# Another written order for a fused scan-attention and feed-forward kernel: scores in 20 places of TensorE's stream, not 44

## The chip, the cores and the metric

One NeuronCore of one Trainium2 chip runs the whole program; nothing is split over cores. The metric is the device time of one execution in microseconds (us), taken as the median of three runs. Engines: PE is TensorE (PEld its weight load), DVE is VectorE, ACT is ScalarE, POOL is GpSimd, SP is SyncE, whose queue issues nearly all DMAs.

## What is computed

A chunked linear attention with decay, then two feed-forward layers. In the reference's own terms, cut to what matters:

```python
for c in range(nc):                       # chunks of the sequence
    cum = np.cumsum(la, axis=-1)
    L = np.exp(cum[:, :, :, None] - cum[:, :, None, :]) * causal
    CB = np.einsum('bhin,bhjn->bhij', Cc, Bc)             # the scores
    y_intra = np.einsum('bhij,bhjd->bhid', CB * L, xc)
    y_inter = np.einsum('bhin,bhnd->bhid', Cc, state) * decay_to_i[:, :, :, None]
    y[:, :, sl] = y_intra + y_inter
    state = decay_full[:, :, None, None] * state + np.sum(Bx, axis=2)
h = np.maximum(np.maximum(x @ w1, x @ w2), x @ w3);  x = h @ w_out      # 256 -> 768 -> 256
gate = 1 / (1 + np.exp(-(x @ w_gate)));  out = gate * (x @ w_val) @ w_out   # 256 -> 1536 -> 256
```

There are 4 batches, 8 heads and 768 positions, so 3072 tokens of 256 features. Inputs are float32.

## The kernel before

The sequence is cut into 8 chunks of 96 positions, and the 32 pairs of batch and head into 8 groups of four, so the attention has 64 steps k = 8c + g. Each step is a **score** (`score`, L344 to L356), a **weighing** (`weigh`, L366 to L376) and, by fours from step 24 on, **outputs** (`outputs`, L378 to L388). A score is four matmuls. For k below 16 they are float32, from operands that ScalarE masks (`mask`, L338 to L341, words `k0` to `k15`); from chunk 2 on they are bfloat16 (L355), on operands `bi` and `cs` split in three parts (words `P`, `Q`) and spread by DMAs (words `Pd`). A score lands in a PSUM tile of the pool `psu`, which has three tiles under one tag, `up`. DVE's weighing (word `m`) multiplies it by the decay factors, and so frees the PSUM tile. The decay factors of two steps share a tile `dec`; it is loaded (word `Ld`) and turned into factors by two scans on DVE (words `D..a`, `D..b`, L303). `dec0` and `dec1` come from the input; the later ones come from a clipped copy `ad` that the kernel makes at its start (words `a`, `clip`, `astore`). Four buffers hold `dec` tiles, so load n waits for the weighings of tile n - 4. The scan needs a constant in PSUM, `delta`, which ACT copies (L273).

Outputs (word `y`, L385) are matmuls of 32 columns each. ACT rounds their result (`high`, word `H`), DVE takes the rest (`low`, word `X`), and four transposes on DVE (`turn`, word `T`) bring the state to the next chunk.

The first feed-forward layer runs beside the attention, on tiles of 512 tokens. Every float32 product is three matmuls on high and low halves of its operands. A word `G` issues the terms (high and low weight, high activation), a word `F` the third (low activation). So a `G` with its `F` is six matmuls of 512 columns (in the trace `u<-xt_hi` x4 and `u<-xt_lo` x2), into one PSUM tile of the same three. `E` (ACT), `U` and `V` (DVE) take the maximum over the three products and so free their tiles, `h` and `l` split it, and `N`, `O` are the six matmuls of the down projection (`o<-hi`, `o<-lo`). The words `Lwa`, `sga`, `rawa`, `stta`, `ra`, `adda`, `hia`, `loa` load and decode this layer's weights.

What is written by hand is `ORDER` (L52), a text of such words. `in_order` (L714) emits word after word, and ties each engine's instructions of a word behind that engine's instructions of the words before it. So the text fixes the order on every engine and on SP's queue, and between engines only data, semaphores and buffers decide. `ON_DVE` (L105) lists the words among `adda`, `loa`, `l` and `Q` that DVE does; the others of these kinds go to POOL. After the text come the last products of the first layer and the whole second layer (`ug`, `uv`, `o<-hi,w_d`), whose code isn't part of the change.

```python
def weigh(k):
    ...
        last[0] = dve.tensor_tensor(out=m[:, :, 0:CH], in0=ps[:, :, 0:CH], in1=dc[:, :, 1:LW],
                                    op=ALU.mult)
```

Of the kernel before, what the change touches and what calls it, by code (L numbers as in the profile page):

```python
# [52 lines left out]
LB0 K Lwa00#0 a clip LC0 pk delta Lwa00 sga00 rawa00 stta00 Ld0 clip0 k6 Ld1 k2 k4 D0b S2 ra00 k5  # L53
clip1 D1a m2 adda00 I0 astore hia00 Lb2 P20 k0 D0a k1 I1 I2 Lx00#0 Lx00 bx2 Q20 k3 D1b Ld2 D2b I3
I4 I5 I6 LC1 S0 m0 S3 k7 bx3 m3 bx0 S1 m1 P21 Ld3 S5 m5 k9 I7 k8 D2a bx1 Lwa01#0 Lwa01 k13 k11 S7
loa00 D3a D3b m7 Lx01#0 sga01 rawa01 S4 m4 S6 m6 y3 Q21 Lwa10#0 Lx01 bx4 stta01 ra01 y4 Ld4 D4a y0
y2 y1 H00 X00 D4b I8 I9 Lwa10 bx7 sga10 rawa10 stta10 k14 I10 I11 LB1 I12 k10 adda01 Ld5 bx5 y5
Lx10#0 Lx10 y7 bx6 y6 H01 Lwa11#0 Lwa11 D5b bx11 D5a S11 S10 m11 S9 ra10 S8 T00 bx10 m10 y11 y10
adda10 Ld6 hia01 m9 bx9 y9 m8 hia10 bx8 y8 H10 Ld7 sga11 rawa11 X01 ra11 Lwa20#0 Lwa20 sga20 X10
loa10 loa01 Lwa21#0 Lwa21 D7a rawa20 D6b S13 m13 G000 F000 G001 F001 stta11 adda11 E00 sga21  # L60
rawa21 U00 ra20 Lwa30#0 Lwa30 stta20 stta21 Lx11#0 Lx11 G002 F002 G010 F010 hia11 loa11 ra21 k12
Lwa31#0 sga30 Lwa31 V00 G011 F011 G012 F012 E01 D7b bx14 h00 adda20 bx15 S12 rawa30 U01 V01 Ld8
l00 hia20 Ld9 ra30 sga31 Lx20#0 Lx20 adda21 stta30 D6a hia21 m12 Lwa41#0 loa20 rawa31 ra31 N00 O00
stta31 loa21 Lwa40#0 Lwa40 adda30 hia30 G020 F020 loa30 adda31 G021 F021 P22 k15 G022 F022 T10 h01
D8a E02 U02 bx16 V02 Lwa41 sga41 Lwa50#0 Lwa50 sga40 S14 m14 rawa40 ra40 stta40 l01 hia31 adda40
hia40 Pd21#0 S15 rawa41 loa31 G030 F030 h02 bx12 E03 Pd22#0 Pd22 N01 O01 T01 bx13 D9a bx18 G031
F031 Pd21#1 m15 y15 y13 Pd21#2 ra41 D8b bx17 sga50 l02 stta41 adda41 rawa50 ra50 stta50 loa40 U03
hia41 y12 G032 F032 N02 O02 Pd20#0 Pd20#1 Pd20#2 Pd20#3 D9b V03 Pd20#4 G040 F040 loa41 Pd20 E04
Pd21 S19 m19 S17 m17 y14 Ld10 Lwa51#0 h03 S16 G041 F041 m16 adda50 hia50 loa50 Lwa51 sga51 rawa51
D10a l03 Lx21#0 Lx21 Ld11 Lx31#0 U04 S20 m20 ra51 G042 F042 V04 h04 S18 m18 G050 F050 E05 N03 O03  # L70
S22 Lb3 stta51 S23 adda51 hia51 bx19 y18 y16 D11a Ld12 D10b bx21 m22 loa51 y17 D11b m23 y19 H11
X11 G051 F051 S21 P30 G052 F052 l04 T11 bx23 y23 Lx31 m21 bx22 H20 X20 y21 U05 bx20 y20 y22 H21
Lx30#0 X21 Q30 V05 h05 Lx30 Pd30#0 D12a bx24 Lx41#0 Lx41 N04 O04 D12b bx25 Pd30#1 Pd30#2 G100 F100
T20 G101 F101 P31 Q31 E10 U10 G102 F102 V10 P32 l05 G110 F110 E11 N05 O05 f0 Pd30#3 Ld13 Ld14 D13b
D14a D13a G111 F111 h10 G112 F112 G120 F120 l10 N10 O10 U11 V11 G121 F121 h11 l11 Pd30#4 Pd30 bx27
E12 Pd32#0 Pd31#0 Pd31#1 Pd31#2 Pd31 Pd32 S27 m27 Lb4 U12 P40 G122 F122 V12 S24 D14b Pd40#0 bx29
m24 Q40 G130 F130 N11 O11 h12 l12 G131 F131 S25 m25 E13 G132 F132 U13 V13 S26 h13 l13 P41 Pd40#1
Pd40#2 Pd40#3 m26 N12 O12 Ld15 D15a D15b bx26 G140 F140 E14 S28 m28 G141 F141 Ld16 bx31 bx28 T21
Lx40#0 Q41 Pd40#4 bx30 P42 S29 G142 F142 U14 Lx40 m29 V14 S30 m30 G150 F150 E15 Ld17 D17a S31
Pd42#0 Pd42 G151 F151 Ld18 Pd40 y27 H30 m31 bx34 y31 H31 X31 D18b X30 D16a U15 G152 F152 Pd41#0  # L80
h14 l14 N13 O13 V15 h15 Ld19 D19b D16b D19a D18a G200 F200 E20 N14 O14 G201 F201 U20 G202 F202
bx33 Pd41#1 Pd41#2 bx32 Pd41 S33 m33 l15 N15 O15 Lb5 P50 Q50 P51 Pd51#0 bx37 Pd50#0 V20 G210 F210
E21 h20 l20 Q51 Pd51#1 T31 S32 m32 T30 Pd50#1 G211 F211 Ld20 S34 m34 f1 U21 G212 F212 V21 Pd51#2
bx36 S37 m37 D17b Lx51#0 G220 F220 E22 h21 l21 S35 m35 Lx50#0 G221 F221 U22 P52 S38 m38 N20 O20
G222 F222 S36 D20b D20a V22 h22 m36 G230 F230 E23 bx35 y35 H40 G231 F231 U23 Pd51 S39 G232 F232
Pd52#0 Pd50#2 Ld21 Pd50#3 m39 Pd50#4 Pd50 Lx50 bx38 l22 X40 bx40 bx39 V23 N21 O21 h23 Pd52 G240
F240 E24 S42 D21a m42 D21b N22 O22 Lb6 P60 Q60 G241 F241 U24 Lx51 S41 bx42 m41 P61 G242 F242 V24
h24 Ld22 Ld23 Pd60#0 Pd60#1 l23 Pd60#2 S40 m40 G250 F250 E25 S43 G251 F251 bx41 D22a m43 T40
Pd60#3 y39 H41 X41 Pd61#0 bx43 y43 H50 X50 G252 F252 Pd61#1 N23 O23 D22b Ld24 l24 Q61 U25 V25
Pd61#2 G300 F300 S45 m45 G301 F301 N24 O24 Ld25 D24a Lx60#0 bx45 P62 h25 l25 Pd62#0 Pd62 Pd60#4  # L90
D23a E30 U30 G302 F302 V30 S44 m44 N25 O25 G310 F310 D25b D23b S47 bx46 m47 D24b h30 Pd60 G311
F311 E31 U31 S46 m46 Lb7 bx44 Pd61 l30 G312 F312 Ld26 V31 P70 f2 bx47 S51 m51 G320 F320 h31 Pd70#0
Pd70#1 Q70 Pd70#2 Pd70#3 Pd70#4 Lx60 S49 P71 G321 F321 T41 D25a Ld27 y47 E32 m49 U32 Q71 P72 bx50
# [880 lines left out]
```

## Time and profile before

| | |
|---|---|
| median of three runs | 546.75 us (545.62 to 547.71) |
| the profiled execution | 546.38 us, its span 544.6 us |
| busy in the span | PE 523.3 us (96%), PEld 418.2, DVE 401.1 (74%), ACT 313.8, POOL 90.4 |
| chain that ended last | PE 82%, DVE 7%, DMA 5%, ACT 3%, issue 2% |
| granted TensorE clock | 1.00 over the span |

Attention and the first layer take the span up to about 208 us, the second layer the rest. A group of matmuls in the timeline has the start of its first one and the time to the end of its last one; matmuls overlap, so the pace of PE is read from one group's start to the next one's, not from the second column. A row of the waits says which engine and line stood idle, until whose work, for how many us in total, how often, and the longest. "issue" means that no wait is visible.

### The profile page before, as it was taken

Reading aid. Unit: us, or ns where it says so; the run is one execution under the profiler, and the core shown is the slowest. Engines: PE = TensorE matmul, PEld = TensorE weight load, DVE = VectorE, ACT = ScalarE, POOL = GpSimd, SP = SyncE. Lnnn points to the kernel's source line nnn. Section 1 sums busy time; section 2 is a strip of 40 time slices with the busy share of each in tenths; the row PEclk is TensorE's granted clock in tenths of the full one; section 3 lists DMA queues with packets and bytes.
Section 4 is the critical chain, followed back from the end, with each engine's and each line's share of the span. In section 5 each row is a group of like instructions: output and inputs, shape, how many; then the busy total and the mean of one; then the engine's idle time right before and its main releaser. Section 6 shows DMA issues by size and latency. Waiting matters only on the chain.

```text
span 544.6 us, 7902 instructions
## 1 busy us (share of the span) xinstructions
PE 523.3 (96%) x2897; PEld 418.2 (77%) x2898; DVE 401.1 (74%) x682; ACT 313.8 (58%) x551; POOL 90.4 (17%) x127
## 2 busy tenths in 40 slices
...
GB/s 209 289 308 214 211 158 164 162 151 138 204 182 139 222 17 201 186 46 148 78 40 0 2 0 1 1 40 39 2 0 1 0 1 78 1 0 0 2 0 78
DMA packets 33895, 50.53 MB, mean 93 GB/s; under 512 B 3392, under 2 KB 19904, under 8 KB 33856
## 3 DMA queue, kind: packets, MB, share of 16 engines
...
## 4 chain that ended last, share of the span: by engine, by line
PE 82%; DVE 7%; DMA 5%; ACT 3%; issue 2%; SPq 0%; POOL 0%; DVEq 0%; POOLq 0%; ACTq 0%
PE u L461 22%; PE o L851 17%; PE ug L820 15%; PE uv L820 15%; PE o L461 7%; PE y L385 2%; PE s L352 2%; DVE dec L303 2%; PE s L355 1%; DMA bc<-in_bch 1%; DMA bx<-in_bn 1%; DMA dec<-ad 1%; DVE t_a L609 1%; DVE mt L375 1%; DVE s L644 1%
## 5 line engine op out<-in xcount | busy, mean ns | idle before, releaser
L461 PE MATMUL u<-xt_hi,w_a 128*128 128x512 f32 x432 | 121.6, 402 | 1.7 <-DVE w_a L618 0.5
L820 PE MATMUL ug<-xt_hi,w_g 128*128 128x512 f32 x252 | 92.0, 390 | 0.3 <-ACT ug L823 0.2
L461 PEld LDWEIGHTS u<-xt_hi,w_a 128*128 128x128 f32 x432 | 77.3, 188 | 19.0 <-DVE w_a L618 1.4
L820 PE MATMUL uv<-xt_hi,w_v 128*128 128x512 f32 x252 | 91.1, 390 | 0.0
L851 PE MATMUL o<-hi,w_d 128*128 128x512 f32 x288 | 78.4, 389 | 0.0
L461 PE MATMUL u<-xt_lo,w_a 128*128 128x512 f32 x216 | 66.9, 391 | 0.4 <-DVE xt_lo L402 0.4
L303 DVE TENSOR_TENSOR_SCAN dec<-dec,delta 128x388 f32<-128x388 f32 x64 | 59.5, 949 | 4.5 <-DMA dec<-ad 4.3
L851 PEld LDWEIGHTS o<-hi,w_d 128*128 128x128 f32 x288 | 54.1, 188 | 11.3
L895 DVE TENSOR_TENSOR lo<-y,hi 128x512 fp32r<-128x512 f32 x72 | 49.2, 687 | 16.1 <-ACT hi L894 15.2
L820 PEld LDWEIGHTS ug<-xt_hi,w_g 128*128 128x128 f32 x252 | 47.3, 188 | 11.2 <-ACT ug L823 0.7
L820 PEld LDWEIGHTS uv<-xt_hi,w_v 128*128 128x128 f32 x252 | 47.3, 188 | 10.7 <-DVE y L828 0.4
L894 ACT CAST hi<-y 128x512 fp32r<-128x512 f32 x72 | 44.5, 620 | 13.2 <-DVE y L891 12.0
L820 PE MATMUL ug<-xt_lo,w_g 128*128 128x512 f32 x126 | 49.1, 389 | 0.0
L820 PE MATMUL uv<-xt_lo,w_v 128*128 128x512 f32 x126 | 49.0, 389 | 0.0
L891 DVE TENSOR_TENSOR y<-uv,y 128x512 f32<-128x512 f32 x36 | 24.8, 688 | 32.9 <-PE uv L820 32.5
L461 PEld LDWEIGHTS u<-xt_lo,w_a 128*128 128x128 f32 x216 | 40.5, 188 | 9.7 <-DVE xt_lo L402 0.9
L851 PE MATMUL o<-lo,w_d 128*128 128x512 f32 x144 | 45.6, 391 | 0.0
L825 ACT COPY sv<-uv 128x512 f32<-128x512 f32 x36 | 21.2, 588 | 34.9 <-PE uv L820 34.7
L375 DVE TENSOR_TENSOR mt<-s,dec 128x384 f32<-128x384 f32 x64 | 34.6, 549 | 8.8 <-PE s L355 7.2
L644 DVE TENSOR_TENSOR s<-u,s 128x512 f32<-128x512 f32 x50 | 34.1, 682 | 8.4 <-PE u L461 7.3
L828 DVE TENSOR_TENSOR y<-ug,y 128x512 f32<-128x512 f32 x36 | 24.8, 689 | 21.0 <-ACT y L825 15.0
L461 PE MATMUL o<-hi,w_a 128*128 128x512 f32 x144 | 39.6, 397 | 0.0
(107 smaller groups left out, 808.7 us busy)
## 6 DMA issues: line engine op xcount, KB each, us to landing
...
```

Source lines behind the costliest of these rows:

```text
L303: dve.tensor_tensor_scan(out=f, data0=f, data1=delta.rearrange("p u w -> p (u w)"), initial=0.0, op0=ALU.mult, op1=ALU.add)
L352: pe.matmul(ps[:, q, 0:CH], bcf[c][:, 128 * q:128 * q + 128], cm[:, k % MASKED, q], start=True, stop=True)
L375: last[0] = dve.tensor_tensor(out=m[:, :, 0:CH], in0=ps[:, :, 0:CH], in1=dc[:, :, 1:LW], op=ALU.mult)
L461: pe.matmul(ps, w[int(e == 1)], a_lo if e == 2 else a_hi, start=start, stop=stop)
L644: evict[1] = dve.tensor_tensor(out=s, in0=banks_of[t, m, 1 + (kind == "V")], in1=s, op=ALU.max)
L820: turn[0] = pe.matmul(ps, w, x, start=new and e == 0, stop=e == 2, skip_group_check=not new)
L825: evict[0] = act.copy(self.temp(1 if i == 6 else 2), ps)
L828: evict[1] = dve.tensor_tensor(out=self.t[k], in0=ps, in1=self.t[k], op=ALU.add)
L851: turn[0] = pe.matmul(acc2[t][d], w, x, start=n == 1 and e == 0, stop=n == M2 and e == 2)
L891: evict[1] = dve.tensor_tensor(out=g, in0=v, in1=g, op=ALU.mult)
L894: act.copy(hl[0], g)
L895: dve.tensor_tensor(out=hl[1], in0=g, in1=hl[0].bitcast(F32), op=ALU.subtract)
```

## The change

A new text `ORDER` and a new list `ON_DVE`. No function, size, tile or product changes. A few rows of the text:

```diff
-LB0 K Lwa00#0 a clip LC0 pk delta Lwa00 sga00 rawa00 stta00 Ld0 clip0 k6 Ld1 k2 k4 D0b S2 ra00 k5
-clip1 D1a m2 adda00 I0 astore hia00 Lb2 P20 k0 D0a k1 I1 I2 Lx00#0 Lx00 bx2 Q20 k3 D1b Ld2 D2b I3
+a Lwa00#0 K I0 I1 Ld0 Lwa00 sga00 clip0 pk clip I2 rawa00 stta00 LC0 k0 LB0 k3 delta D0b k4 D0a
+astore S0 Lx00#0 Lx00 bx1 Ld1 k7 k1 ra00 m0 I3 I4 I5 I6 I7 I8 adda00 hia00 clip1 D1b I9 D1a bx2
...
-ON_DVE = """Q20 loa10 adda20 adda21 loa21 adda40 l02 loa40 l05 l10 l11 l12 l21 l25 l35""".split()
+ON_DVE = """adda20 adda21 adda30 loa21 loa30 adda40 loa40 loa50 l04 Q31 l21 Q60 Q61 l23 l31 l34 l35""".split()
```

By the instruction order as built, the bfloat16 scores stood in 44 places of PE's stream with float32 products between them, and now stand in 20. Outputs that stand between scores of one place are counted with it. The three excerpts below are of that order; where an instruction is issued four times in a row, one row of it is shown.

First, TensorE in the fifth chunk. `s5_2` is the score of chunk 5, group 2; `u3_2_4_0` is a product of token tile 2; `o6_2_0` belongs to the down projection; `y1`, `y0` are outputs. Before:

```order
L355 MATMUL s5_2_1593<-cs5_1370,bi1_97 128x96
L461 MATMUL o6_2_0_1484<-hi3_2_2_1448,w_a21_538 128x512
...
L461 MATMUL u3_2_4_1_1613<-xt_hi_92,w_a40_623 128x512 x4
L461 MATMUL u3_2_4_1_1613<-xt_lo_93,w_a40_623 128x512 x2
L355 MATMUL s5_1_1622<-cs5_1370,bi1_97 128x96
L461 MATMUL u3_2_4_2_1630<-xt_hi_92,w_a41_695 128x512 x4
L461 MATMUL u3_2_4_2_1630<-xt_lo_93,w_a41_695 128x512 x2
L355 MATMUL s5_0_1647<-cs5_1370,bi1_97 128x96
L461 MATMUL u3_2_5_0_1656<-xt_hi_92,w_a50_770 128x512 x4
L461 MATMUL u3_2_5_0_1656<-xt_lo_93,w_a50_770 128x512 x2
L355 MATMUL s5_3_1664<-cs5_1370,bi1_97 128x96
```

and now:

```order
L460 MATMUL u3_2_4_2_1624<-xt_hi_92,w_a41_688 128x512 x4
L460 MATMUL u3_2_4_2_1624<-xt_lo_93,w_a41_688 128x512 x2
L460 MATMUL o6_2_0_1445<-hi3_2_3_1495,w_a31_620 128x512
...
L354 MATMUL s5_1_1639<-cs5_1362,bi1_97 128x96
L354 MATMUL s5_2_1645<-cs5_1362,bi1_97 128x96
L354 MATMUL s5_0_1651<-cs5_1362,bi1_97 128x96
L384 MATMUL y1_107<-mt7_105,xs4_1_1024 32x112 x4
...
L354 MATMUL s5_3_1677<-cs5_1362,bi1_97 128x96
L460 MATMUL u3_2_5_0_1690<-xt_hi_92,w_a50_702 128x512 x4
```

The four scores of that group, each alone between products before, stand around one set of outputs.

Second, SP's queue at the start of the program. `y1` is the scratch that takes the first chunk's B (512 columns) and C (384 columns), `a4` the decay input for the copy `ad`. Before:

```order
L576 DMA y1_91<-in_bch 128x512
L593 DMA raw_a00_137<-in_w1 128x2x256
L680 DMA a4_110<-in_ah 64x388
L574 DMA y1_91<-in_bch 128x384
L678 DMA pk_109<-in_pick 128x8
L593 DMA raw_a00_137<-in_w2 128x2x256
L287 DMA dec0_149<-in_ah 128x776
L287 DMA dec1_153<-in_ah 128x776
L683 DMA ad_108<-a4_110 64x388
```

and now:

```order
L679 DMA a4_110<-in_ah 64x388
L592 DMA raw_a00_112<-in_w1 128x2x256
L286 DMA dec0_142<-in_ah 128x776
L592 DMA raw_a00_112<-in_w2 128x2x256
L677 DMA pk_109<-in_pick 128x8
L573 DMA y1_91<-in_bch 128x384
L575 DMA y1_91<-in_bch 128x512
L682 DMA ad_108<-a4_110 64x388
...
L286 DMA dec1_172<-in_ah 128x776
```

`dec0` is the third load, not the seventh; B and C come after it; `dec1` comes after the store of `ad` and the first inputs x. On DVE the clip of `a4` now stands behind the clip of `dec0`, and on ACT the copy of `delta` behind the first weight and two masks.

Third, SP's queue where `dec17` to `dec19` are loaded; `cs4`, `bi0` are the spread operands of chunk 4. Before:

```order
L287 DMA dec16_1185<-ad_108 128x776
L294 DMA xs4_0_1193<-in_xh 128x512
L666 DMA cs4_1075<-parts4_1074 16x8x384
L294 DMA bx4_0_1194<-in_bn 128x256
L287 DMA dec17_1233<-ad_108 128x776
L666 DMA bi0_96<-parts4_1074 16x8x512
L666 DMA cs4_1075<-parts4_1074 16x8x384
L287 DMA dec18_1250<-ad_108 128x776
L666 DMA cs4_1075<-parts4_1074 16x8x384
L666 DMA bi0_96<-parts4_1074 16x8x512
L287 DMA dec19_1312<-ad_108 128x776
```

and now:

```order
L286 DMA dec16_1166<-ad_108 128x776
L665 DMA cs4_946<-parts4_945 16x8x384
L293 DMA xs5_0_1217<-in_xh 128x512
L293 DMA bx4_1_1025<-in_bn 128x256
L665 DMA bi0_96<-parts4_945 16x8x512
L286 DMA dec17_1263<-ad_108 128x776
L286 DMA dec18_1311<-ad_108 128x776
L286 DMA dec19_1314<-ad_108 128x776
```

The three loads stand together, ahead of the last spreading DMAs of chunk 4 instead of among them.

## Rows read from the trace of the kernel before

**Rows 1.** Busy time by stretch: from 11 us, from 77.6 us.

```profile
core 0: us, PE busy (x) PEld busy (x) DVE busy (x) ACT busy (x) POOL busy (x), PEclk, DMA share, GB/s
11.00:77.60 66.60, 61.30 (x487) 46.64 (x491) 63.72 (x101) 45.41 (x77) 39.38 (x48) 1.00 0.83 239
77.60:208.80 131.20, 128.98 (x961) 98.11 (x953) 104.07 (x180) 44.73 (x73) 46.33 (x63) 1.00 0.70 148
```

**Rows 2.** Waits of the weight load, 77.6 to 209 us: total, times, longest.

```profile
PEld L355 <- issue: 11.0, 38, 1.1
```

**Rows 3.** TensorE's timeline, 82 to 104 us: start, us, engine, line, operation.

```profile
83.43 1.07 PE L461 MATMUL u<-xt_hi,w_a 128*128 128x512 f32 x4
...
84.79 1.07 PE L461 MATMUL o<-hi,w_a 128*128 128x512 f32 x4
...
94.68 0.35 PE L355 MATMUL s<-cs,bi 96*128 96x96 bf16 x4
94.85 1.17 PE L461 MATMUL u<-xt_hi,w_a 128*128 128x512 f32 x4
...
96.30 1.07 PE L461 MATMUL o<-hi,w_a 128*128 128x512 f32 x4
```

**Rows 4.** TensorE's timeline, 186 to 212 us: two scores together, outputs.

```profile
198.39 0.51 PE L355 MATMUL s<-cs,bi 96*128 96x96 bf16 x8
198.73 1.17 PE L461 MATMUL u<-xt_hi,w_a 128*128 128x512 f32 x4
...
200.20 0.35 PE L355 MATMUL s<-cs,bi 96*128 96x96 bf16 x4
...
205.34 0.34 PE L355 MATMUL s<-cs,bi 96*128 96x96 bf16 x4
205.61 0.97 PE L385 MATMUL y<-mt,xs 128*32 128x112 f32 x32
206.52 1.20 PE L461 MATMUL u<-xt_hi,w_a 128*128 128x512 f32 x4
...
208.10 0.97 PE L385 MATMUL y<-mt,xs 128*32 128x112 f32 x32
```

**Rows 5.** TensorE's timeline, 104 to 131 us: two outputs in one stop, waits.

```profile
110.66 1.74 PE L385 MATMUL y<-mt,xs 128*32 128x112 f32 x64
112.33 1.20 PE L461 MATMUL u<-xt_hi,w_a 128*128 128x512 f32 x4
...
116.69 0.73 PE L461 MATMUL u<-xt_lo,w_a 128*128 128x512 f32 x2 [0.45 <-DVE xt_lo L402]
...
128.96 0.33 PE L355 MATMUL s<-cs,bi 96*128 96x96 bf16 x4 [1.03 <-DVE mt L375]
129.56 1.21 PE L461 MATMUL u<-xt_hi,w_a 128*128 128x512 f32 x4 [0.27 <-DVE s L644]
```

**Rows 6.** DVE's timeline, 111 to 131 us.

```profile
115.23 0.96 DVE L303 TENSOR_TENSOR_SCAN dec<-dec,delta 128x388 f32<-128x388 f32 x1 [1.70 <-DMA dec<-ad]
...
118.80 3.51 DVE L303 TENSOR_TENSOR_SCAN dec<-dec,delta 128x388 f32<-128x388 f32 x4
```

**Rows 7.** SP's timeline, 104 to 114 us.

```profile
111.24 0.54 SPq L287 DMA_DIRECT2D dec<-ad  x1
```

**Rows 8.** All engines' timeline, 0 to 36 us.

```profile
4.57 0.49 ACT L273 COPY delta<-delta_s 128x388 f32<-128x388 f32 x1 [2.17 <-POOL delta_s L271]
...
6.91 0.78 ACT L189 ACTIVATE sg<-raw_a 128x512 f16<-128x512 f32 x1 [1.86 <-DMA raw_a<-in_w]
7.72 0.65 ACT L603 ACTIVATE raw_a<-raw_a 128x512 f32<-128x512 f32 x1
8.28 1.61 ACT L341 ACTIVATE y<-y,pk 128x384 f32<-128x384 f32 x3
...
11.08 1.19 DVE L652 TENSOR_SCALAR dec<-dec 128x768 f32<-128x768 f32 x1 [1.93 <-DMA dec<-in_ah]
...
12.30 0.96 DVE L303 TENSOR_TENSOR_SCAN dec<-dec,delta 128x388 f32<-128x388 f32 x1
```

More of the change, by code (lines that the diff above doesn't have):

```diff
@@ L52 @@
 ORDER = """
[L53 to L93, printed above, removed]
@@ L100 @@
-h35 l35 S62 D31a m62 G402 F402 S60 m60 N35 O35 bx61 T60 S59 bx63 m59 V40 bx62 y63 H71 X71 y59 H70
-X70
+a Lwa00#0 K I0 I1 Ld0 Lwa00 sga00 clip0 pk clip I2 rawa00 stta00 LC0 k0 LB0 k3 delta D0b k4 D0a
+astore S0 Lx00#0 Lx00 bx1 Ld1 k7 k1 ra00 m0 I3 I4 I5 I6 I7 I8 adda00 hia00 clip1 D1b I9 D1a bx2
+Ld2 D2a Lb2 S3 m3 S1 m1 Lwa01#0 Lwa01 D2b k2 S2 m2 k6 P20 k5 S5 m5 sga01 rawa01 bx3 LC1 k10 S7 k15
+Ld3 bx0 Ld4 y0 Lx01#0 stta01 loa00 Q20 y2 D3b m7 Lx01 ra01 adda01 hia01 k8 S6 k14 D3a bx6 LB1 k13
+bx7 y3 m6 loa01 y1 S4 Ld5 m4 D4a S10 bx5 Lx10#0 Lx10 k9 S9 bx4 y4 P21 D4b Q21 bx9 k12 D5a y6 y5
@@ new lines @@
+rawa40 Pd21#1 hia30 U02 D7a G022 F022 ra31 S15 h01 Lx11#0 Lx11 Lwa50#0 Ld8 stta40 loa30 V02 P22
+Ld9 adda31 D8a ra40 S14 Lx20#0 N01 D9a m15 h02 l01 Lwa41#0 Lwa41 hia31 bx13 m14 Lwa50 sga50 O01
+adda40 bx12 Pd21#2 Pd21 sga41 T01 G030 loa31 D8b F030 E03 rawa41 stta41 hia40 loa40 Lx20 ra41 bx16
+G031 F031 G032 F032 N02 l02 O02 adda41 rawa50 ra50 stta50 adda50 hia41 G040 F040 D9b Pd22#0 hia50
+y13 Pd20#0 Pd20#1 U03 bx14 y14 y12 V03 T10 Pd22 E04 bx15 y15 H11 loa41 Pd20#2 Pd20#3 Pd20#4 Pd20
+S16 h03 bx19 S19 m19 m16 G041 l03 F041 X11 U04 loa50 G042 Lwa51#0 Lwa51 sga51 S18 S17 m18 rawa51
```

43 lines of the change are left out of this document (37 added, 6 removed).

## The prediction

> **What bounds the kernel now.** I read the busy time by stretch first. From 11 to 77.6 us DVE is busy for 63.72 of 66.60 us [rows 1]: it has hardly a gap, and PE, busy for 61.30, takes what DVE releases. From 77.6 to 208.8 us it is the other way round: PE is busy for 128.98 of 131.20 us, DVE for 104.07. So in the first stretch only DVE's chain counts, and a change of PE's own order is worth nothing there. In the second, each tenth of a microsecond on PE is on the path. The second layer, behind both, is not touched. Next I read the weight load's waits in the second stretch: 38 times it stood before a bfloat16 score, for 11.0 us in all, with nothing to be waited for ("issue") [rows 2]. Most of that lies beside running matmuls; what PE itself loses shows only in the timeline's starts. That is the view for every price below.
>
> **What a lone score costs.** Six float32 products without a stop take 84.79 - 83.43 = 1.36 us [rows 3]. From a lone score to the second group after it is 96.30 - 94.68 = 1.62 us; the score's four matmuls take 0.17 of it (94.85 - 94.68), the six products 1.36, so about 0.09 us is lost where float32 begins again, and I take 0.10 to have the slight delay ahead of the score with it. Two scores in one place take 198.73 - 198.39 = 0.34 us, twice 0.17, and the six products after them 200.20 - 198.73 = 1.47, so 0.11 is lost once [rows 4]. The loss belongs to the stop, not to the score.
>
> **Term 1, stops removed.** Of the 40 scores of chunks 3 to 7, which lie in the second stretch, the order before has 38 lone or paired stops between products (and one beside outputs), as many as the row of the weight load counts [rows 2]. The new order has 7 such stops, and 8 in which the scores stand directly beside outputs. For the 31 that go I take 0.11 each: -3.4 us (bounds 0.09 and 0.11: -2.8 to -3.4). For chunk 2's scores, in the first stretch, I take nothing: DVE covers them.
>
> **Term 2, scores beside outputs.** PE pays for a change of tile at the outputs anyway. Score to outputs takes 205.61 - 205.34 = 0.27 us, 0.10 over the score's 0.17, which is what outputs after a product cost too (term 3) [rows 4]. So a score there adds next to nothing; I take 0.03 for each of 8 (bounds 0 and 0.10): +0.2, at most +0.8.
>
> **Term 3, more stops for outputs.** From chunk 3 on the old order takes the ten sets of outputs in 7 stops, three of them with two sets; the new one in 9, with one pair. Two sets in one stop take 112.33 - 110.66 = 1.67 us [rows 5], one alone 206.52 - 205.61 = 0.91, so a split costs 0.15. Six products between two stops for outputs take 208.10 - 206.52 = 1.58, that is 0.22 more than without [rows 4]. Two more stops: 2 x 0.37 = +0.7 us.
>
> **Term 4, waits in the second stretch.** Three waits stand out before: 0.45, 1.03 and 0.27 us [rows 5], 1.75 together. Their cause is one: a scan waited 1.70 us for its tile, and the next one started at 118.80 though its load was issued at 111.24, 7.6 us earlier [rows 6, 7]; behind it four scans ran in a row for 3.51 us, and the maxima and weighings that free PSUM tiles came late. In the new order the loads of `dec17` to `dec19` are issued together. Their buffers come free with the weighings of chunk 3, and on PE five products (6.8 us at 1.36), one set of outputs (0.9) and down projections (2.3, being ten matmuls at 1.36 for six) lie between these and the scans: 10.0 us for 7.6. I let the three waits go: -1.75. New ones will come. Two or three scores in one place need two or three of the three PSUM tiles, each freed only by DVE, while the old order asked for one at a time. The nearest price is the worst wait shown, 1.03 + 0.27 at one stop; the lowest is none. I take 0.08 at each of the 15 stops, +1.2 (bounds 0 and 3.3), nearer to none, because the text spreads the weighings so that in most places some 1.2 us of PE's work lies between a tile's last matmul and its next use, against 0.9 for a maximum (0.66 for L644 [rows 6], and some 0.2 around it, an estimate).
>
> **Term 5, the head.** What counts here is when DVE's chain starts and how long it is. Up to the weighing of step 21, the last of chunk 2, both orders give DVE 89 instructions, with the same 24 scans, 24 weighings, 12 decodes and 10 maxima; the lists differ by one add and one subtraction for another two of about the same size. So only the start counts. The clip of `dec0` began at 11.08, after 1.93 us of waiting for it, the first scan at 12.30 [rows 8]. Now `dec0` is asked for earlier, but the scan also needs `delta`, which was copied at 4.57 and now stands behind the decode of the first weight and two masks. If that weight comes as before, ACT reaches the copy at 8.37 (7.72 + 0.65), plus 1.07 for two of three masks in 1.61, and ends it 0.49 later, at 9.9: 2.4 us sooner. But the weight's second half now waits behind `dec0` in the queue, and `dec0` came 4.2 us after that half before (11.08 - 6.91) [rows 8]; with this added, `delta` is there at 14.1, or 1.8 late. `dec1`, B, C and the copy `ad` are asked for later as well. Between a gain of 2.4 and a loss of 1.8 I take 0, and 1.5 either way for the range.
>
> **The sum.** -3.4 + 0.2 + 0.7 - 1.75 + 1.2 + 0 = -3.05 us on the profiled execution's 546.38: 543.3. The median of the runs is 546.75, 0.4 above it, so a median near 543.5 would fit; I say **543.4**. All bounds at their good ends give 546.38 - 3.4 + 0.7 - 1.75 - 1.5 = 540.4, all at their bad ends, the three waits kept, 546.38 - 2.8 + 0.8 + 0.7 + 3.3 + 1.5 = 549.9.
>
> **A rule against it.** The rows say that every return from a bfloat16 score to products costs 0.09 to 0.11 us, with no change of PE's tiling (a score spans the array's 128 columns, as a product does) [rows 3, 4]. The Trainium skill, TensorEngine Tiling (Array Packing), Key Properties, says that changing the tiling mode drains TensorE and names no such cost for a change of number format. By that rule only the outputs' stops would count: term 1 would be 0, term 3 would stay, and the time would be 546.38 + 0.7 - 1.75 + 1.2 = 546.5. That is a rival of its own below; the rows speak against it.
>
> **Rivals.**
> - *PSUM tiles take back the gain, slower.* A stop of two or three scores is right after a product whose maximum isn't done, and DVE has a scan of 0.96 [rows 6] in front of a weighing. One mechanism, at the 15 grouped stops; it takes back the whole gain at 0.28 us a stop ((3.05 + 1.2) / 15) and makes the kernel measurably slower from 0.47. At 0.50: 546.38 - 4.25 + 7.5 = 549.6. For it: the one wait of that kind before cost 1.30 at one stop [rows 5]. Against: DVE has 27 us to spare in this stretch [rows 1].
> - *The waits only move.* DVE's scans still wait for loads somewhere, 1.75 us as before: 545.0, or with 1 us lost in the head 546.0. For it: SP's queue is one file, and a load that waits for its buffer holds up all behind it. Against: the distance worked out in term 4.
> - *More than forecast.* The head starts 1.5 sooner and no new waits come: 543.3 - 1.5 - 1.2 = 540.6.
> - *The rule on tiling:* 546.5.
>
> **How the numbers follow.** What a measurement of this kernel can tell is about 0.5%, 2.7 us: faster means below 544.0, slower above 549.5. The forecast has 0.52, waits that move 0.23, more than forecast 0.12, slower 0.10, the rule 0.03. Of the forecast I put five sixths below 544.0: faster 0.43 + 0.12 = 0.55, rounded up for part of the moved waits to 0.56; slower 0.10; within 0.5% the remaining 0.34. The range runs from 540.4 to 547.6: it holds the forecast, the moved waits and the rule, and leaves out the slower case and some of the better one.
>
> **What would show it.** In the new profile the stretch from the end of the head to the last outputs should have some 15 stops, in which groups of x8 or x12 bfloat16 matmuls stand, each followed by one long first product; the weight load's row "issue" before L355 should fall from 38 times to about 15. The wait of 1.70 us before a scan and PE's 1.03 before a score should be gone. DVE should stay full until PE takes over, near 77 us. I'd be wrong if PE's waits for L375 or L644 at the grouped stops add up to over 3 us, if the first scan starts after 14 us and DVE's full stretch ends as much later, or if a return to products after a grouped stop costs more than after a lone one.

## The result, and the profile after

The change makes the kernel slower by 0.7%: 550.13 us (547.0 to 553.55, 19 runs) against 546.27 us (544.7 to 548.52, 19 runs), a ratio of 1.007 (95% interval 1.005 to 1.0091). The forecast was 543.4, faster; the range ended at 547.6. The profiled execution of the changed kernel took 548.08 us, its span 546.2.

The page of the new order, busy time and the chain that ended last:

```profile
PE 521.2 (95%) x2895; PEld 419.6 (77%) x2895; DVE 401.7 (74%) x684; ACT 313.5 (57%) x551; POOL 85.8 (16%) x125
...
PE 69%; DMA 12%; DVE 12%; issue 3%; ACT 2%; POOL 1%; SPq 0%; DVEq 0%; POOLq 0%; ACTq 0%
```

Engines do the same work; the chain doesn't. PE had 82% of it, and now has 69%; DMA and DVE have 12% each, where they had 5 and 7. The waits of the stretch in which PE is the bound, 76 to 206 or 207 us (total, times, longest), first the weight load's, then PE's, DVE's and those of SP's queue:

```profile
PEld L354 <- issue: 5.6, 23, 0.4
...
PE u L460 <- DVE s L643: 3.6, 3, 2.1
PE u L460 <- DVE mt L374: 0.7, 2, 0.5
...
DVE dec L302 <- DMA dec<-ad: 8.4, 6, 2.1
...
SPq L286 <- POOL mt L363: 14.4, 7, 5.0
...
SPq L286 <- DVE mt L374: 8.1, 3, 4.7
```

and the old order's row for DVE, 76 to 207 us:

```profile
DVE dec L303 <- DMA dec<-ad: 4.3, 4, 1.7
```

The stops went: 38 waits of the weight load before a score [rows 2] are 23. I had said about 15; the 15 places are there, seven of them count a second time behind their outputs, and one wait lies inside a place. But DVE waits twice as long for decay tiles, and PE, in whose way only single waits of up to 1.03 us stood [rows 5], now waits 2.1 us for a maximum at one place. The rows of SP's queue show, too, that a load doesn't wait for weighings alone: POOL multiplies B by the decay factors (word `bx`, L363), reads the same tile, and is waited for longer (14.4 us) than the weighings (8.1). The same stretch in busy time [rows 1]:

```profile
76.00:206.00 130.00, 123.63 (x941) 96.07 (x932) 105.21 (x181) 41.73 (x69) 41.35 (x60) 1.00 0.72 148
```

PE is idle for 6.4 of 130 us, where it was idle for 2.2 of 131.2.

**Where along the program.** I counted in both traces the work that PE had done (0.2266 us for a matmul of 512 columns, 0.165 for one of a float32 score, which is between the 0.21 and 0.11 that it takes at the two paces of the head, 0.0425 for one of a bfloat16 score, 0.0284 for one of outputs) and took the time less this work. After 60 us of work, near 78 us, the new order is 2.3 us ahead; after 136 us of work, near 160, still 2.3. Between the two points the old order has 24 stops for scores or outputs and the new one nine, and yet the lead doesn't grow: 5.8 us are lost there before, 5.7 now. (The old order's words stand there in e1, e3, e10, e11 and e18 as well, and their traces lose 6.4 to 7.8; so single executions differ by more than these stops are worth.) Then, in the last 32 us of work, in which chunks 6 and 7 are done, it loses 6.5 us to the old order's 2.3, and comes out 1.8 behind. That last stretch is the same in all runs below and can be compared:

| profiled executions | us lost on PE in the last 32 us of work |
|---|---|
| old end, four `dec` buffers: before, e1, e2, e11, e16, e18 | 2.3 to 2.4 |
| old end, five buffers: e10, e12 | 2.5, 2.4 |
| new end, four buffers: after, e3, e5, e6, e7, e9, e13, e14 | 6.5, 4.5, 4.0, 4.4, 6.8, 7.8, 7.7, 5.6 |
| new end, five buffers: e4, e8, e15 | 4.7, 2.9, 3.4 |

The place at which the new order loses most, on SP, DVE and PE:

```profile
175.29 5.61 SPq L286 DMA_DIRECT2D dec<-ad  x2
180.99 2.07 SPq L665 DMA_DIRECT2D bi<-parts  x2
...
179.49 1.02 DVE L374 TENSOR_TENSOR mt<-s,dec 128x384 f32<-128x384 f32 x2
...
186.60 0.96 DVE L302 TENSOR_TENSOR_SCAN dec<-dec,delta 128x388 f32<-128x388 f32 x1 [2.12 <-DMA dec<-ad]
187.48 1.26 DVE L427 STREAM_TRANSPOSE xs<-y 32x128 f32<-32x128 f32 x4
188.75 0.96 DVE L302 TENSOR_TENSOR_SCAN dec<-dec,delta 128x388 f32<-128x388 f32 x1
189.63 1.46 DVE L643 TENSOR_TENSOR s<-u,s 128x512 f32<-128x512 f32 x2
...
163.78 1.19 PE L460 MATMUL u<-xt_hi,w_a 128*128 128x512 f32 x4 [0.36 <-DVE s L643]
...
187.61 0.61 PE L460 MATMUL o<-lo,w_a 128*128 128x512 f32 x2
190.35 1.21 PE L460 MATMUL u<-xt_hi,w_a 128*128 128x512 f32 x4 [2.13 <-DVE s L643]
191.40 1.09 PE L460 MATMUL u<-xt_lo,w_a 128*128 128x512 f32 x4
...
197.18 1.17 PE L460 MATMUL u<-xt_hi,w_a 128*128 128x512 f32 x4 [0.68 <-ACT hi L645]
```

SP's first row holds two loads. The first, of `dec29`, goes out at 175.29, the second, of `dec30`, only at 180.58: its buffer is that of `dec26`, and the weighing of step 52, the last to read it, is the second of the two at 179.49 to 180.51. The tile lands at 186.51. Its scan `D30a` stands in the new text ahead of a turn, a scan and two maxima (`D30a T51 D28b ... U34 V34`), so DVE stands still for 2.12 us, the maxima start at 189.63, and PE, which has no free PSUM tile, waits. In the old text the same scan stands behind these maxima. There its load is issued at 180.47, as late, and nobody waits: at 187.13 the turn runs, at 188.44 the two maxima.

Not all of PE's new waits come from loads. The 0.36 us at 163.78 and the 0.68 at 197.18 (for ACT's `h`) stand in the traces with five `dec` buffers as well (e4, e8, e15), and so does a wait of 0.57 for POOL's `l` at 141.37. Together they are 1.6 us, and the old order has none of them.

A second loss doesn't show in this execution. The trace belongs to one in which the granted clock was 1.00 throughout; in most of the 19 the mean over the span was less, and the time goes with it: 547.6 to 549.4 us for the four at 1.000, 547.0 to 550.4 for eight at 0.994 to 0.997, 550.1 to 553.6 for seven at 0.983 to 0.992. Of the 137 runs of the old order beside the experiments none is below 0.995. By the four alone (median 548.55) the loss would be 2.3 us, not 3.9.

### The profile page after: what moved, and what is told of

The parts are those of the page before. It is cut to its first block, busy times and chain, and to the rows that moved or that the text cites. A ratio compares the mean times of both kernels' runs of the same rounds, so it can differ in the third digit from the quotient of the medians.

```text
span 546.2 us, 7898 instructions
## 1 busy us (share of the span) xinstructions
PE 521.2 (95%) x2895; PEld 419.6 (77%) x2895; DVE 401.7 (74%) x684; ACT 313.5 (57%) x551; POOL 85.8 (16%) x125
## 3 DMA queue, kind: packets, MB, share of 16 engines
HBM read 38.51 MB, written 3.25 MB: 76 GB/s over the span
## 4 chain that ended last, share of the span: by engine, by line
PE 69%; DMA 12%; DVE 12%; issue 3%; ACT 2%; POOL 1%; SPq 0%; DVEq 0%; POOLq 0%; ACTq 0%
PE o L850 17%; PE ug L819 15%; PE u L460 15%; PE uv L819 15%; PE o L460 5%; DMA dec<-ad 5%; DVE dec L302 4%; DVE mt L374 3%; DVE s L643 2%; DMA xs<-in_xh 2%; DVE xs L427 2%; DMA bc<-in_bch 1%; DMA bi<-parts 1%; DMA raw_a<-in_w 1%; DMA dec<-in_ah 1%
## 5 line engine op out<-in xcount | busy, mean ns | idle before, releaser
L460 PE MATMUL u<-xt_hi,w_a 128*128 128x512 f32 x432 | 116.8, 396 | 6.3 <-DVE s L643 3.6
L460 PEld LDWEIGHTS u<-xt_hi,w_a 128*128 128x128 f32 x432 | 79.2, 188 | 26.9 <-DVE s L643 5.1
L460 PE MATMUL u<-xt_lo,w_a 128*128 128x512 f32 x216 | 65.3, 391 | 0.0
L641 ACT COPY s<-u 128x512 f32<-128x512 f32 x25 | 14.6, 586 | 49.6 <-PE u L460 49.6
L827 DVE TENSOR_TENSOR y<-ug,y 128x512 f32<-128x512 f32 x36 | 24.8, 689 | 21.0 <-ACT y L824 14.8
```

The source lines that it names most:

```text
L460: pe.matmul(ps, w[int(e == 1)], a_lo if e == 2 else a_hi, start=start, stop=stop)
L641: evict[0] = act.copy(s, banks_of[t, m, 0])
L827: evict[1] = dve.tensor_tensor(out=self.t[k], in0=ps, in1=self.t[k], op=ALU.add)
```

## The experiments

All were timed in five rounds, with the old order beside them on the same chip: e1 to e4 on one, e5 to e8, e9 to e12, e13 to e16, and e17 with e18 on others. Chips differ by as much as the smaller effects, so medians are compared within such a group. The idle products of e5 and others produce nothing that is used; e11 leaves six of them out.

### Which part of the text: e1 to e4

Each hybrid takes the first words from one text, and the other words in the order of the other text; a word's engine is that of the text it comes from.

```diff
 # e1_new_head: new[:320] + old order of the rest   (cut ahead of S16, chunk 2)
 # e2_old_end:  new[:720] + old order of the rest   (cut in token tile 2)
 # e3_new_end:  old[:719] + new order of the rest
 # e4_five_dec: the new order, with
-DECS = 4
+DECS = 5
-    a4 = acon.tile([NC * NP * 2, 4, LW], F32, name="a4")
+    a4 = flat[0:NC * NP * 2, 4864:4864 + 4 * LW].rearrange("p (u w) -> p u w", u=4)
```

> The new text up to the first score of chunk 2 (320 words), then the old text's remaining words in the old order; each word's engine is that of the text it comes from. The new profile was about 2.3 us ahead of the old one from there on, until 163 us. If the lead is the head's and can be kept, this takes 546.3 - 2.3 = 544.0 us, and the first product starts near 32.9 us, not 34.9. If loads in the last chunks set the end, whoever comes early only waits longer for them: 546 again. If the head gave nothing and the lead came from stops removed: 546.3.

> The new text up to the last products of token tile 2 (720 words: head, and the grouped scores of chunks 2 to 4), then the old text's rest (chunks 5 to 7). Theory of the late loads (the loss lies only in the new text's last part, where scans wait for their tiles and maxima stand behind them): the lead of 2.3 us stays, 544.0 us. Rival, the PSUM tiles of grouped stops (a loss at every group): no better than e1, the grouped chunks cost what they save or more, 545 to 547. Rival, loads of chunk 7 set the end whoever comes early: 546.

> The reverse: the old text up to the last products of token tile 2 (719 words), then the new text's rest. Theory of the late loads: the whole loss of the new order is here, 4 us, so 546.3 + 4 = 550.3 us. PSUM tiles at every group: only the 7 or so stops of the last part count of 15, so about half of the 4 us: 548. If the old first part, being 2.3 us later, gives the loads more time: 546.3 + 1.7 = 548 as well, but then with scans that wait less than 1 us in the last part.

> The new order with five buffers for the decay tiles, not four; the clipped input a4 moves into the free end of the scratch y1 to make room. Loads 20 to 31 then wait for weighings of one tile earlier. Theory of the late loads: DVE's waits for dec in 76 to 206 us fall from 8.4 to under 3, the 2.13 us wait of a product for a maximum at 190 us goes, and the time is 546 to 547.5. PSUM tiles of grouped stops: DVE may wait less but PE's waits stay, 549.5 to 550.5. If DMA bandwidth, not the buffers, makes the loads late: issues come earlier, landings not, 549 to 550.

| | median us | ratio (95%) | mean clock 0.998 and up / 0.994 to 0.997 / below |
|---|---|---|---|
| e1 | 550.75 | 1.008 (1.0051 to 1.011) | 0 / 2 / 4 of 6 |
| e2 | 547.39 | 1.0008 (0.9987 to 1.0029) | 1 / 4 / 7 of 12 |
| e3 | 549.92 | 1.0082 (1.0064 to 1.0101) | 6 / 0 / 0 of 6 |
| e4 | 545.62 | 1.0003 (0.9981 to 1.0025) | 6 / 2 / 4 of 12 |

The times of e3 and e4 came out as the theory of the late loads has it: the new end alone costs 3.8 us (546.1 before), with the old head and a full clock, and with a fifth buffer the new order's ratio to the old one is 1.0003, not 1.007, some 3.7 us less. The waits came out less well. In e3's trace DVE waits 4.0 us for decay tiles, no more than in the old order's (4.3), and the product that waits 2.13 us above waits 0.35. So e3 shows where the loss is, and not that late loads make it. In e4's trace DVE waits 6.0 us, where under 3 were expected, and that product 1.0, where no wait was expected; the load of `dec30` goes out at 175.15, 5.4 us sooner, but lands at 184.16, only 2.3 sooner, so the rival of the bandwidth has its part. The waits of 76 to 207 us in e4:

```profile
DVE dec L302 <- DMA dec<-ad: 6.0, 7, 1.6
...
PE u L460 <- DVE s L643: 1.8, 3, 1.0
```

e1 and e2 missed all numbers. No theory on record had a term for what their runs show: a mean clock below 0.993 in 11 of 18. All three with the new head have such runs, e3, with the old head, has none. So the head has a loss of its own.

### What the new head does to the clock: e5, e9, e11, e13, e14

In the new order PE stands idle at 17 to 19 us, between the scores of steps 2 and 5. ACT is behind it: the copy `P20` waits 2.67 us for chunk 2's B and C, and the mask `k5` that the score needs stands behind `P20`. TensorE and ACT in the new order's trace:

```profile
13.79 3.29 PE L351 MATMUL s<-y 128*128 128x96 f32 x24
19.11 2.02 PE L351 MATMUL s<-y 128*128 128x96 f32 x16 [2.03 <-ACT y L340]
...
33.09 1.20 PE L460 MATMUL u<-xt_hi,w_a 128*128 128x512 f32 x4 [0.60 <-ACT xt_hi L397]
...
9.35 0.47 ACT L272 COPY delta<-delta_s 128x388 f32<-128x388 f32 x1
...
17.60 0.94 ACT L670 CAST parts<-bc 128x896 bf16<-128x896 f32 x1 [2.67 <-DMA bc<-in_bch]
18.45 0.61 ACT L340 ACTIVATE y<-y,pk 128x384 f32<-128x384 f32 x1
```

```diff
 # e5_no_gap, and with ten words for four e9_gap_filled and e14_filled_same_chip (one kernel)
-... m2 k6 P20 k5 S5 ...
+... m2 k6 I10 I11 I12 I13 P20 k5 S5 ...
 # e11_old_with_gap: the old order
-... k1 I1 I2 Lx00 ... D2b I3 I4 I5 I6 LC1 S0 ...
+... k1 Lx00 ... D2b LC1 S0 ...
 # e13_new_same_chip: the new order unchanged
```

> The new order with four more idle products between the scores of steps 2 and 5, where PE stood idle from 16.98 to 19.11 us; four take some 1.82 us (seven took 3.19), so nothing should be pushed. Theory of the clock (in many executions the granted clock falls to half from about 20 us to 24 or 33 us, because of this gap): every run's mean clock is 0.998 or more, and the median falls from 550.1 to about 548.5, where the runs of the new order at 1.000 lie. Rival (the clock falls by chance or for the idle time before 9 us): runs at 0.983 to 0.997 stay, and the median stays at 550.

> The new order with ten idle products, not four, in the gap between the scores of steps 2 and 5. In e5 the four took only 1.03 us (0.22 each) and left 1.3 to 1.7 us idle, and 4 of 12 runs still showed a clock under 0.998. Theory of the clock: ten take 2.2 us, the gap is full, 10 or more of 12 runs lie at 0.998 or more, and the ratio to before is 0.995 to 0.999. Rival (the share of low clocks is chance): a third of the runs stay under 0.998 and the ratio is e5's or higher, because ten products may push the score behind them by 0.2.

> Reverse of e5 and e9: the old order without the six idle products I1 to I6, which leaves PE idle for some 3 us between the first two scores; nothing else changes, and they produce nothing that is used. Theory of the clock: many runs fall to 0.983 to 0.997 as in the new order, and the median rises by 1.5 to 4 us. Rival (the clock of the new order falls for another reason): all runs stay at 0.998 or more and the time is the old one, 0 to 0.3 us less.

> The new order unchanged, as the base of this call. Theory (late loads in the last part, and a clock that falls in the head and behind the stall at 190 us): a ratio to before of 1.005 to 1.009, with a third or more of the runs under 0.993. If chips differ as much as e5 and e9 did, anything from 1.000 to 1.009, and then e14 to e16 are read against this one.

> e13 with ten idle products in the head's gap (the kernel of e9). Theory of the clock in the head: no run under 0.994, and the median 1 to 2 us under e13's. Rival (e9's 1.0048 says that the gap costs nothing): within 0.5 us of e13.

| | median us | ratio (95%) | clock 0.998 and up / 0.994 to 0.997 / below |
|---|---|---|---|
| e5, four idle products | 546.87 | 0.9988 (0.9968 to 1.0009) | 8 / 3 / 1 of 12 |
| e9, ten | 548.76 | 1.0048 (1.0024 to 1.0071) | 6 / 4 / 0 of 10 |
| e13, none | 553.5 | 1.0115 (1.0091 to 1.014) | 0 / 0 / 6 of 6 |
| e14, ten, same chip as e13 | 548.84 | 1.0045 (1.0029 to 1.006) | 9 / 3 / 0 of 12 |
| e11, the old order with a gap | 547.97 | 1.0034 (1.0016 to 1.0051) | 12 / 0 / 0 of 12 |

e13 and e14 ran on one chip and settle it: with the gap filled no run is below 0.995, and the median is 4.7 us lower, where 1 to 2 were expected (e13's own ratio is over the 1.005 to 1.009 expected). The two heads by 5 us (the column behind POOL's is the granted clock), and PE's timeline, first of e13:

```profile
15.00:20.00 5.00, 2.10 (x20) 1.94 (x18) 4.58 (x7) 1.95 (x4) 2.12 (x5) 1.00 0.84 311
20.00:25.00 5.00, 5.00 (x39) 4.50 (x40) 4.40 (x7) 2.94 (x5) 2.79 (x2) 0.60 0.84 240
25.00:30.00 5.00, 5.00 (x36) 4.50 (x36) 2.11 (x4) 4.72 (x9) 3.70 (x7) 0.50 1.00 352
30.00:35.00 5.00, 5.00 (x57) 4.73 (x56) 4.95 (x10) 2.19 (x4) 1.84 (x5) 0.87 1.10 290
...
19.94 2.75 PE L351 MATMUL s<-y 128*128 128x96 f32 x16 [2.90 <-ACT y L340]
...
26.39 5.24 PE L351 MATMUL s<-y 128*128 128x96 f32 x24
```

and of e14:

```profile
15.00:20.00 5.00, 4.95 (x36) 3.88 (x36) 4.97 (x8) 3.90 (x7) 2.65 (x6) 1.00 0.71 272
20.00:25.00 5.00, 4.53 (x61) 3.84 (x59) 4.72 (x8) 3.35 (x6) 2.66 (x3) 1.00 0.92 236
...
17.29 2.32 PE L705 MATMUL idle<-delta_s 128*128 128x512 bf16 x9
...
28.45 3.00 PE L351 MATMUL s<-y 128*128 128x96 f32 x24
```

In e13 PE was busy for 2.10 of 5 us and idle for 2.90 at a stretch; from some 21 us the clock is at its lower level (0.50, 1.2 GHz of 2.4) for some ten us, and 24 score matmuls take 5.24 us for 3.00. Whether the fall comes differs from run to run: the profiled run of the new order had the gap of 2.03 us and no fall.

e5 and e9 didn't agree with each other on two chips; within their own groups they say only that fewer runs fall. e11 missed: its gap of 2.50 us was at 12 to 14.5 us, where score matmuls still take double time in the old order too (last section), so there was no full pace to lose. It became slower for a reason that I left open. Its trace is 0.5 us ahead of the old order's until 72 us of work and 1.3 behind at 88, with a score at 93.51 us that waits 0.87 for a DMA of `bc`. The old order's trace doesn't have this wait, but those of e1, e3, e17 and e18, which have the old words there, do, with 0.56 to 0.79 us; so it doesn't come from the gap.

Of the remaining falls, 0.994 to 0.997, two have a trace (e7, e9), and in both the clock falls behind the stall of the last part. e9's execution at 0.996, by 5 us, and PE behind the stall:

```profile
185.00:190.00 5.00, 5.00 (x24) 3.98 (x23) 3.20 (x6) 0.85 (x2) 0.00 (x0) 1.00 1.03 165
190.00:195.00 5.00, 3.17 (x10) 2.28 (x9) 4.80 (x12) 0.40 (x2) 2.97 (x6) 0.80 0.41 99
195.00:200.00 5.00, 5.00 (x56) 3.52 (x55) 3.96 (x6) 1.65 (x3) 0.59 (x1) 0.85 0.26 79
...
192.44 1.58 PE L460 MATMUL u<-xt_hi,w_a 128*128 128x512 f32 x4 [1.83 <-DVE s L643]
193.82 1.91 PE L460 MATMUL u<-xt_lo,w_a 128*128 128x512 f32 x4
```

Four products that take 0.91 us elsewhere take 1.38 and 1.71 there. So a stall of two us can cost a second time. Not every small fall comes from it: e16, whose old end has no such stall, has four runs at 0.995 and 0.996.

### Which load, and is it the buffers: e6, e7, e8, e10, e15, e16

```diff
 # e6_scan_later: e5 with
-Ld30 D30a T51 D28b ... U34 V34 O31
+Ld30 T51 D28b ... U34 V34 D30a O31
 # e7_load_sooner: e5 with
-Lb7 P70 Q70 Pd70 ... S48 bx47 bx51 S50 m50 Lx61 Lx61 Ld27
+Lb7 bx47 P70 Q70 Ld27 Pd70 ... S48 bx51 S50 m50 Lx61 Lx61
 # e8_no_gap_five: e5 with DECS = 5;  e10_before_five: the old order with DECS = 5 (a4 moved as in e4)
 # e15_filled_five: e14 with DECS = 5;  e16_filled_old_end: e2 with the ten idle products
```

> e5 with one word moved: the first scan of decay tile 30 stands behind the two maxima of token tile 3, m = 4 (U34, V34), not ahead of a turn, a scan and these. Its load is issued as before. Theory of the late loads (a scan that waits for its tile holds up the maxima behind it in DVE's line): the 2.13 us wait of a product for a maximum at 190 us falls to under 0.4, and the time is 1.5 to 2 us less than e5's. Rival (the maximum would be late anyway, since the turn and the scan ahead of it or PE's own order set it): under 0.5 us less.

> e5 with two words moved: POOL's bx47, the last reader of decay tile 23, stands ahead of the subtraction Q70, and the load of tile 27 stands ahead of chunk 7's spreading DMAs, not behind the first of them and the inputs x. Theory of the late loads: the load is issued near 168.5 us, not 170.65, its scan waits under 0.3 us, not 0.98, and the time is 0.5 to 1.0 us less than e5's. Rival (DMA bandwidth sets the landing): it is issued sooner and lands as late, the time is e5's.

> e5 and five decay buffers together (with a4 in the free end of y1). If the two losses are separate and add: 548.5 - 4.3 = 544.2 us with the clock at 0.998 or more in every run, faster than before by 1.8 to 2. If the gap doesn't set the clock: as e4, 545.6, with runs at 549. If the idle products delay the head: 545 or more at full clock.

> Control: the old order with five decay buffers, and a4 in the free end of y1. Theory of the late loads in the new order's end: the old order has products to spare there and waits 4.3 us for dec on DVE, hardly any of it on PE, so it gains under 1 us (ratio 0.998 to 1.001), while the new order gained 4.3 at full clock. Rival (a fifth buffer helps any order, and tells nothing of the change): 4 us as well, 542.

> e14 with five decay buffers. Theory of the late loads: 3 to 4 us less than e14, all runs at 0.997 or more, because the stall behind which the clock falls is gone as well; a ratio of 0.995 to 0.998. Rival (DMA bandwidth, not buffers): within 1 us of e14.

> e14 with the old text from the last products of token tile 2 on, four decay buffers. Theory: as e15, 3 to 4 us less than e14, since the old end asks for its loads with products to spare; 543.5 to 545, a ratio of 0.994 to 0.998. Rival (the old end only gains because of a fifth buffer in e12): 546 or more.

| | median us | ratio (95%) | against |
|---|---|---|---|
| e6 | 548.11 | 1.001 (0.9988 to 1.0032) | e5 546.87 |
| e7 | 547.53 | 1.0017 (0.9995 to 1.004) | e5 546.87 |
| e8 | 545.38 | 0.9986 (0.9962 to 1.001) | e5 546.87 |
| e10 | 547.46 | 1.0016 (1.0002 to 1.003) | before 546.37 |
| e15 | 546.53 | 1.0001 (0.9984 to 1.0019) | e14 548.84 |
| e16 | 545.89 | 0.9991 (0.9975 to 1.0008) | e14 548.84 |

On one chip, e14 to e16: with the gap filled, five buffers take 2.4 us (by the ratios), the old end 2.95. For both 3 to 4 were expected, and e16's 545.89 lies over the 543.5 to 545 expected. The control e10 gains nothing from a fifth buffer and loses 1.1 us, so a fifth buffer isn't good for every order. e8 missed: 544.2 with every run at 0.998 or more was expected, four of its 12 runs are lower, and by the ratios (0.9986 and 0.9988) it is as fast as e5, by the medians 1.5 us faster. So on that chip the fifth buffer isn't shown to bring anything.

e6 and e7 didn't bring the time that was expected; one word at a time doesn't do it. In e6 the wait of 2.13 us is gone. But e5's trace, with which e6 is to be compared, has only 0.42 us of it, and the other traces of the new end with four buffers have 0.35 to 2.32; so its absence in one execution says little. PE waits twice in e6 at stops of scores that had not waited so before:

```profile
193.53 0.33 PE L354 MATMUL s<-cs,bi 96*128 96x96 bf16 x4 [0.76 <-ACT s L641]
...
195.81 0.33 PE L354 MATMUL s<-cs,bi 96*128 96x96 bf16 x4 [0.77 <-DVE s L643]
```

Seven of e6's 12 runs had a clock below 0.993, so its median says little, and the three at 0.998 and more (544.15, 544.8 and 548.04) are too few. That the one scan costs the time is read from a trace; no run shows it. In e7 the load of `dec27` went out at 168.72, not 170.65, landed at 173.30, not 176.80, and its scan no longer waited; the scan of `dec30` then waited 2.29 us. In that execution the later load decided.

### The price of a stop, and the mixtures: e17, e18, e12

```diff
 # e17_more_stops: the old order, a word Z<k> that issues two of the four matmuls of score k
-G132 F132 U13 V13 S26 m26
+G132 Z26 F132 U13 V13 S26 m26
 # e18_head_filled: e1 with the ten idle products
 # e12_mixed: e2 with the ten idle products and DECS = 5
```

> The old order, in which 36 of the 40 scores of chunks 3 to 7 are cut in two: the first two of a score's four matmuls stand between the two words of the product (or down projection) ahead of it, the other two where the score stood. So 36 stops more, no matmul more, and the PSUM tile of a score is taken 0.45 us earlier. Price of the prediction's term 1 (a return from bfloat16 to products loses 0.09 to 0.11 us, and PE is the path there): 36 x 0.09 to 0.11 = +3.2 to +4.0 us, 549.6 to 550.3. The rule on tiling (a change of number format costs nothing, only a change of tiling drains): +0 to 0.5 us. If waits hide stops: +1 to 2.

> e1 (the new text up to the first score of chunk 2, then the old one) with ten idle products in the gap. If the head's lead of some 2 us, with the clock kept, reaches the end: 544 to 545, a ratio of 0.995 to 0.998. If the later part only waits longer for its loads or for DVE: 546 to 547, a ratio of 1.000. e16, with the grouped scores of chunks 2 to 4 on top, had 0.9991.

> e2 (the new text up to token tile 2, then the old rest) with ten idle products in the head's gap and five decay buffers. If head, middle and end add as the theory has it: e2's runs at full clock lie near 543.5; with the clock kept and the fifth buffer, 542.5 to 543.5, a ratio of 0.992 to 0.995 to before. If the gain of the head is taken back by loads that come no sooner: 545 or more at full clock.

e17: 548.98 us, ratio 1.0054 (1.0033 to 1.0074). That is 2.95 us (1.8 to 4.0) for 36 stops, 0.08 each (0.05 to 0.11); 3.2 to 4.0 were expected, and the interval reaches them. Its timeline:

```profile
130.93 0.71 PE L468 MATMUL u<-xt_lo,w_a 128*128 128x512 f32 x2
131.48 0.26 PE L362 MATMUL s<-cs,bi 96*128 96x96 bf16 x2
131.57 1.17 PE L468 MATMUL u<-xt_hi,w_a 128*128 128x512 f32 x4
132.58 0.26 PE L362 MATMUL s<-cs,bi 96*128 96x96 bf16 x2
```

Two products from 130.93 take 0.55 us for 0.45, four from 131.57 take 1.01 for 0.91: 0.10 a return, whatever stands behind.

e18: 546.1, ratio 1.0004 (0.9982 to 1.0026); the seven runs at 0.998 and up have a median of 545.6, five fell lower, in the profiled one at 65 to 71 us, far from the gap. By the seven, the new head alone, its gap filled, brings 0.8 us; by all runs nothing that can be measured.

e12: 545.07, ratio 0.9968 (0.9955 to 0.9981), 11 of 12 runs at 0.998 and up. **It beats both kernels**, the old order by 0.3%; 542.5 to 543.5 was expected. e16 has the same order with four buffers and no measurable gain; the two ran on different chips, so what the fifth buffer is worth there is not settled. e10 and e12, though, ran on one chip, both with five buffers and the old end: the new head, its gap filled, and the grouped scores of chunks 2 to 4 take 2.4 us there (547.46 to 545.07, with intervals that don't meet). That is the one gain from the new order that a run shows clear of noise.

## Why the prediction was wrong

*Terms 1 to 3, the stops: the price is right, their sum isn't seen.* 31 stops went, and the price holds where scores are grouped and where they stand beside outputs. In the new order's trace:

```profile
193.71 0.34 PE L354 MATMUL s<-cs,bi 96*128 96x96 bf16 x4
193.98 0.97 PE L384 MATMUL y<-mt,xs 128*32 128x112 f32 x32
...
202.07 0.68 PE L354 MATMUL s<-cs,bi 96*128 96x96 bf16 x12
202.57 1.17 PE L460 MATMUL o<-hi,w_a 128*128 128x512 f32 x4
203.59 0.59 PE L354 MATMUL s<-cs,bi 96*128 96x96 bf16 x8
```

Twelve score matmuls in 0.50, then four products in 1.02 for 0.91: 0.11 lost, as after one score. Score to outputs takes 0.27, as before [rows 4]. The rival that took its rule from the Trainium skill, TensorEngine Tiling (Array Packing), Key Properties, falls with e17: scores that keep the tiling cost 0.08 a stop on the whole time, where by that rule they would cost nothing.

That it is the change of number format which costs is not shown, however. Where products resume after a wait, with no score between, four of them take 1.03 us at 116.41 and 1.05 at 190.35, for 0.91: 0.12 and more lost, as after a score. So a wait costs about that much over its idle time, and the forecast had no term for it. From 60 to 168 us of work the visible waits of PE are 6.2 us, for 2.2 before, and the new order loses 12.2 us, for 8.1. The waits are thus the whole difference, and the -2.5 us of terms 1 to 3 don't appear in it. Five more waits at 0.12 are 0.6 us of them (an estimate); where the rest went I can't say from one execution.

*Term 4, waits in the second stretch: wrong, and this is the step that failed.* I let three waits go for 1.75 and put new ones at 1.2, spread over the grouped stops as waits for PSUM tiles: -0.55 us in all. The three went, but in the trace PE's visible waits are 6.2 us for 2.2, so +4.0 for the -0.55: 3.7 of them stand behind scans that had waited for their tiles (1.12 at 116.41, 0.49 at 178.57, 2.13 at 190.35), 2.5 elsewhere. I looked at one place, the loads of `dec17` to `dec19`, and there the sum of distances didn't hold either: issued at 104.82 to 106.08, they landed up to 7.9 us later, and the wait only moved to a product at 116.41.

```profile
113.96 1.81 DVE L302 TENSOR_TENSOR_SCAN dec<-dec,delta 128x388 f32<-128x388 f32 x2 [1.41 <-DMA dec<-ad]
115.69 1.46 DVE L643 TENSOR_TENSOR s<-u,s 128x512 f32<-128x512 f32 x2
...
116.41 0.96 PE L460 MATMUL u<-xt_hi,w_a 128*128 128x512 f32 x3 [1.12 <-DVE s L643]
```

The loads behind these I didn't follow, and most of the loss lies where the last five are due: 4.2 us more on PE than in the old order (6.5 for 2.3), 1.0 of it in the two waits that don't depend on loads (0.36 and 0.68). The cause that the trace shows is the one that I had read for the old order, a scan in DVE's line ahead of its tile with maxima behind it [rows 6], and had taken for cured. Shown by runs: the place (e3, e16, and the table of the last 32 us) and the buffers (e15 against e14, and e4, with e10 as control; e8 against e5 doesn't show it). Not shown by a run: that it is this one scan (e6). Bandwidth shares in it: with five buffers `dec30` was asked for 5.4 us sooner and came 2.3 sooner.

*Term 5, the head: wrong in its kind.* I took 0, from 2.4 sooner to 1.8 later. `dec0` came at once, `delta` was copied at 9.35, the first scan began at 9.85 for 12.30 [rows 8], and the first product at 33.09, 2 us sooner. The end sooner of my range was right. What I had no term for is the clock: where the old order has idle products or a score nearly everywhere (its longest gap among the first scores, 0.55 us), the new one has 2 to 3 us, because I read who waits for `delta`, and not who waits behind `P20`. It cost 4.7 us on the chip of e13 and e14; in the 19 runs the median of all is 1.6 us over that of the four at full clock.

*The rivals.* "The waits only move" was the nearest: a load that waits in SP's line, and a scan that waits for it. I priced it by the old order's 1.75 us; it is 2.4 to 3 with the gap filled (e15, e16). "PSUM tiles take back the gain" has the right sign and the wrong mechanism: PE's waits for maxima and weighings add up to 4.3 us, over the 3 that I had named, but 3.25 of them stand at products in the midst of products, behind late scans (116.41, 190.35), and only 1.1 close behind scores (0.24, 0.36 and 0.49). Another 0.33 stand at a score that waited for ACT's copy, which frees a tile too; "each freed only by DVE" was wrong. In e6, two such waits are 1.5 us together. "More than forecast" had the head right and the waits wrong.

*What stays open.* With the gap filled and five buffers (e15) the time is the old order's, 1.0001 (0.9984 to 1.0019), though the head is 2 us ahead and 31 stops are gone; the profiled execution of e15, 544.04 us, is 2.3 under the old order's, its median isn't. That trace still has the three waits that don't depend on loads (0.57, 0.36 and 0.69 us). Only one execution of a kernel has a trace, so I can't say where the others lose it; landings of the same load vary by 1 to 2 us between the traces (`dec30`: 4.5 to 6.6 us with four buffers and the new end).
